# Start-up loads moved to ScalarE's queue and merged, transposes in merged PSUM banks, w2 in three loads: a dense layer with squared ReLU on one core

## Chip, cores, metric

One core of one Trainium2 chip. The metric is the device time of one execution in microseconds. Timed runs of one kernel differ by 0.5 us and more from each other, so comparisons use several runs taken on the same chip in the same rounds.

## The reference

```
h   = einsum("bsd,df->bsf", x, w1) + b1      # x: 1 x 2048 x 576, w1: 576 x 4608
r   = where(h > 0, h, 0)
out = einsum("bsf,fd->bsd", r * r, w2) + b2  # w2: 4608 x 576, everything bf16
```

## The kernel before

The rows of x are worked in four blocks of 512. For block 0, PE (TensorE) itself transposes x, because the first matmuls must start early; the other blocks come through DMA transposes. The contraction length 576 is 4 x 128 + 64. The first four 128-column groups of w1 ("w1n", loaded as four row blocks k = 0 to 3 of 128 KB) are used as full 128-row matmuls of half width (256 columns of x at a time, so that work can begin after two x tiles). The 64 left-over rows ("small rows", w1n8) close those groups. All other groups of w1 ("w1_h") are used in pairs of 64-row matmuls, the "64-row stage".

The parts that matter (cuts are marked):

```
WARM = [512] * 6 + [128]                    # warm-up matmuls on constants
...
load_x(nc.sync, 0)
load_x(nc.scalar, 1)
load_w1n(nc.sync, 0)
load_x(nc.scalar, 2)
load_w1n(nc.sync, 1)
load_x(nc.sync, 3)
for k in range(2, NK):                      # NK = 4
    load_w1n(nc.sync, k)
...
nc.gpsimd.dma_start(out=b1_rows[0:NFT, :], in_=...)   # bias 1
nc.gpsimd.dma_start(out=b2_col[:], in_=...)
...
def x_copies(h):                            # PSUM -> SBUF, half h of block 0
    hc = slice(h * HS, (h + 1) * HS)
    for k in range(NK):
        src = half_banks[h][k][:, 0, :]
        if k % 2 == 0: keep(nc.vector.tensor_copy(out=xT0[:, O + k, hc], in_=src))
        else:          keep(nc.scalar.copy(out=xT0[:, O + k, hc], in_=src))
    keep(nc.vector.tensor_copy(out=xT0[:, E3, hc], in_=half_banks[h][2][:, 1, :]))
...
# part(h, k): 4 half-width matmuls of x half h with w1 block k
for j in range(2):
    for k in range(NK): x_transpose(j, k)
for j in range(2): x_transpose(j, NK)
x_copies(0)
part(0, 0)
for k in range(NK + 1): x_transpose(2, k)
part(0, 1)
part(0, 2)
for k in range(NK + 1): x_transpose(3, k)
x_copies(1)
dup_windows(0)
part(0, 3)
part(1, 0)
make_b1T()                                  # transpose of bias 1
for k in range(1, NK): part(1, k)
...                                         # small rows, then the 64-row stage
for (j0, j1) in [(0, 1), (1, 2), (2, 4), ...]:
    load_w1(nc.sync, 0, j0, j1)
    load_w1(nc.sync, 1, j0, j1)
    if j0 == 0:
        load_w1n8(nc.sync, 0)               # the small rows
        load_w1n8(nc.sync, 1)
...
for c in (0, 2, 1, 3): load_w2(c)
```

Of the kernel before, what the change touches and what calls it, by code (L numbers as in the profile page):

```python
# [11 lines left out]
BF16 = mybir.dt.bfloat16  # L12
FP32 = mybir.dt.float32
# [4 lines left out]
def kernel(  # L18
# [9 lines left out]
    nc = tc.nc  # L28
    keep = tc.keep_in_program_order
    P = 128  # L30
# [3 lines left out]
    S, D = x2.shape  # L34
    F = w1.shape[1]
    NFT = F // P
    NC = D // H
    NK = NC // 2
    G = 4
    GW = G * P  # L40
# [4 lines left out]
    RT = SB // P  # L45
    DT = P
    DM = D - DT

    const = ctx.enter_context(tc.tile_pool(name="const", bufs=1))
# [6 lines left out]
    ps_h = ctx.enter_context(tc.tile_pool(name="ps_h", bufs=4, space=PSUM))  # L56
    ps_o = ctx.enter_context(tc.tile_pool(name="ps_o", bufs=4, space=PSUM))

    wps = ps_o.tile([P, 512], FP32, name="wps", tag="po")
    ones = nc.const_aps.tensor(1.0, [P, 512], BF16)  # L60
    WARM = [512] * 6 + [128]
    for i, n in enumerate(WARM):
        keep(nc.tensor.matmul(wps[:, 0:n], lhsT=ones[:, 0:P], rhs=ones[:, 0:n], start=True, stop=True))  # L63

    xs = const.tile([P, RT, D], BF16, name="x_sb")
    w1n = wpool.tile([P, NK, GW], BF16, name="w1n")
# [4 lines left out]
    def load_x(eng, rt):  # L71
        keep(eng.dma_start(out=xs[:, rt, :], in_=x2[rt * P:(rt + 1) * P, :]))

    def load_w1n(eng, k):
        keep(eng.dma_start(out=w1n[:, k, :], in_=w1[k * P:(k + 1) * P, 0:GW]))

    def load_w1n8(eng, h):
        src = w1[NK * P:D, 0:GW].rearrange("p (i h f) -> p i h f", h=2, f=P)
        keep(eng.dma_start(out=w1n8[h * H:(h + 1) * H, :, :], in_=src[:, :, h, :]))

    def load_w1(eng, h, j0, j1):
        keep(eng.dma_start(out=w1_h[h * H:(h + 1) * H, :, j0 * P:j1 * P],
                      in_=w1_v[:, :, GW + h * FH + j0 * P:GW + h * FH + j1 * P]))

    load_x(nc.sync, 0)
    load_x(nc.scalar, 1)
    load_w1n(nc.sync, 0)
    load_x(nc.scalar, 2)
    load_w1n(nc.sync, 1)
    load_x(nc.sync, 3)  # L90
    for k in range(2, NK):
        load_w1n(nc.sync, k)

    ident = const.tile([P, P], BF16, name="ident")
    make_identity(nc, ident[:])
    b1_rows = const.tile([P, P], BF16, name="b1_rows")
    nc.gpsimd.memset(b1_rows[:], 0.0)
    nc.gpsimd.dma_start(out=b1_rows[0:NFT, :], in_=b1.rearrange("(ft p) -> ft p", p=P))
    b2_col = const.tile([P, 1], BF16, name="b2_col")
    nc.gpsimd.dma_start(out=b2_col[:], in_=b2[DM:D].rearrange("(d o) -> d o", o=1))  # L100
    b2T = const.tile([P, 1], FP32, name="b2T")
    nc.gpsimd.tensor_copy(out=b2T[:], in_=b2_col[:])
    warm = const.tile([P, 1], FP32, name="warm")
    keep(nc.scalar.activation(out=warm[:], in_=nc.const_aps.tensor(0.0, [P, 1], FP32), func=ACT.Relu))

    E3, O, SPC, E = 0, 1, 5, 6
    LO_W = [O, O + 1, O + 2, O + 3, E, E + 1, E + 2, E3, SPC]
# [9 lines left out]
    def dup_windows(sb):  # L117
        xT = xT_blk[sb]
        keep(nc.vector.tensor_copy(out=xT[0:H, SPC:SPC + 4, :], in_=xT[H:P, E3:E3 + 4, :]))  # L119
        keep(nc.vector.tensor_copy(out=xT[H:P, SPC:SPC + 4, :], in_=xT[0:H, O:O + 4, :]))  # L120
# [7 lines left out]

    w2_sb = wpool.tile([P, NFT, D], BF16, name="w2_sb")
    w2_view = w2.rearrange("(ft p) d -> p ft d", p=P)  # L130
    W2CH = 9

    def load_w2(c):
        keep(nc.sync.dma_start(out=w2_sb[:, c * W2CH:(c + 1) * W2CH, :], in_=w2_view[:, c * W2CH:(c + 1) * W2CH, :]))
# [3 lines left out]
    alloc_xT(0)  # L138
    xT0 = xT_blk[0]
    HS = SB // 2  # L140
    tb_po = [ps_o.tile([P, 2, HS], BF16, name="tb", tag="po") for _ in range(2)]
    tb_ph = [ps_h.tile([P, 2, HS], BF16, name="tb", tag="ph") for _ in range(4)]
    half_banks = [tb_ph, None]

    def x_transpose(j, k):
        h, q = divmod(j, 2)
        qc = slice(q * P, (q + 1) * P)
        bank, slot, c0 = (half_banks[h][k], 0, k * P) if k < NK else (half_banks[h][2], 1, D - P)
        keep(nc.tensor.transpose(bank[:, slot, qc], xs[:, j, c0:c0 + P], ident[:]))  # L149

    def x_copies(h):
        hc = slice(h * HS, (h + 1) * HS)
        for k in range(NK):
            src = half_banks[h][k][:, 0, :]
            if k % 2 == 0:
                keep(nc.vector.tensor_copy(out=xT0[:, O + k, hc], in_=src))  # L156
            else:
                keep(nc.scalar.copy(out=xT0[:, O + k, hc], in_=src))
        keep(nc.vector.tensor_copy(out=xT0[:, E3, hc], in_=half_banks[h][2][:, 1, :]))


    b1T = const.tile([P, NFT], FP32, name="b1T")

    def make_b1T():
        b1T_ps = ps_o.tile([P, P], BF16, name="b1T_ps", tag="po")
        keep(nc.tensor.transpose(b1T_ps[:], b1_rows[:], ident[:]))  # L166
        keep(nc.vector.tensor_copy(out=b1T[:], in_=b1T_ps[:, 0:NFT]))

# [26 lines left out]
    def a_full(sb, order):  # L195
        xT = xT_blk[sb]
        banks = []
        for g in range(G):
            pool, tag = (ps_o, "po") if g < 2 else (ps_h, "ph")
            banks.append(pool.tile([P, SB], FP32, name="pn", tag=tag))  # L200

        def pair(i, start, stop):
            keep(nc.tensor.matmul(banks[2 * i][:], lhsT=w1n8[0:H, i, :], rhs=xT[0:H, SPC, :],  # L203
                             start=start, stop=stop, skip_group_check=order == "k_outer"))
            keep(nc.tensor.matmul(banks[2 * i + 1][:], lhsT=w1n8[H:P, i, :], rhs=xT[H:P, E3, :],  # L205
                             start=start, stop=stop, skip_group_check=order == "k_outer"))

        def full(g, k, start, stop):
            keep(nc.tensor.matmul(banks[g][:], lhsT=w1n[:, k, g * P:(g + 1) * P], rhs=xT[:, O + k, :],  # L209
                             start=start, stop=stop))  # L210

        if order == "rows_first":
            for i in (1, 0):
                pair(i, True, False)
            for g in (2, 3, 0, 1):
                for k in range(NK):
                    full(g, k, False, k == NK - 1)
                evac_h(sb, banks[g], g)
        else:
            if order == "k_outer":  # L220
                tb_new = [ps_h.tile([P, 2, HS], BF16, name="tb", tag="ph") for _ in range(2)]
                half_banks[1] = tb_new + tb_po

                def part(h, k):
                    hc = slice(h * HS, (h + 1) * HS)
                    for g in range(G):
                        keep(nc.tensor.matmul(banks[g][:, hc], lhsT=w1n[:, k, g * P:(g + 1) * P],  # L227
                                              rhs=xT[:, O + k, hc], start=(h == 0 and k == 0), stop=False,
                                              skip_group_check=True))

                for j in range(2):
                    for k in range(NK):
                        x_transpose(j, k)
                for j in range(2):
                    x_transpose(j, NK)
                x_copies(0)
                part(0, 0)
                for k in range(NK + 1):
                    x_transpose(2, k)
                part(0, 1)  # L240
                part(0, 2)
                for k in range(NK + 1):
                    x_transpose(3, k)
                x_copies(1)
                dup_windows(0)
                part(0, 3)
                part(1, 0)
                make_b1T()
                for k in range(1, NK):
                    part(1, k)  # L250
            else:
                for g in (2, 3, 0, 1):
                    for k in range(NK):
                        full(g, k, k == 0, False)
            for i in (1, 0):
                pair(i, False, True)
                evac_h(sb, banks[2 * i], 2 * i)
                evac_h(sb, banks[2 * i + 1], 2 * i + 1)
# [35 lines left out]
    for (j0, j1) in [(0, 1), (1, 2), (2, 4), (4, 6), (6, 8), (8, 10), (10, 12)]:  # L294
        load_w1(nc.sync, 0, j0, j1)
        load_w1(nc.sync, 1, j0, j1)
        if j0 == 0:
            load_w1n8(nc.sync, 0)
            load_w1n8(nc.sync, 1)
    load_xT(1)  # L300
    for (j0, j1) in [(12, 14), (14, 16)]:
        load_w1(nc.sync, 0, j0, j1)
        load_w1(nc.sync, 1, j0, j1)
    keep(nc.sync.dma_start(out=b2_bc[:], in_=b2.partition_broadcast(P)))
    for c in (0, 2, 1, 3):
        load_w2(c)
    load_xT(2)

    alloc_hT(0)
    a_full(0, "k_outer")  # L310
    a_rows(0, 12, 1)
    alloc_hT(1)
# [47 lines left out]
```

## Time and profile before

| | before |
|---|---|
| time, median of the first 3 runs | 290.84 us (290.69 to 291.06) |
| the profiled execution | 291.46 us, span 289.6 us |
| PE busy | 285.5 us, 99% |
| x tile 0 lands / first transpose | 3.72 / 3.77 us |
| w1 block 2 lands / first used (PE's weight load) | 6.47 / 6.69 us |
| w1 block 3 lands / first used (PE's weight load) | 7.05 / 7.46 us |
| first matmul of the 64-row stage on w1_h | 10.29 us |

Busy time of each engine, then the chain of work that ended last by engine, both from the page of before:

```profile
PE 285.5 (99%) x2027; PEld 139.9 (48%) x2032; DVE 78.6 (27%) x176; ACT 96.7 (33%) x154; POOL 2.3 (1%) x10
...
PE 98%; DMA 1%; issue 0%; DVE 0%
```

PE is the bound, so a gain must come from the start, where PE is not yet at work or works slowly. The chain of before in the first 11 us (cut at both ends; columns: start in us, length in us, what; it counts a matmul from the end of the one before, so its times lie up to 0.2 us after the starts that the text names):

```profile
0.73 2.99 DMA x_sb<-in_x_dram
3.73 0.04 issue
3.77 1.25 PE tb L149 x10
5.02 0.86 PE pn L227 x4
5.88 0.53 PE tb L149 x5
6.42 0.98 PE pn L227 x8
7.40 0.28 PE tb L149 x5
7.68 0.87 PE pn L227 x8
8.55 0.06 PE b1T_ps L166
8.61 1.31 PE pn L227 x12
9.92 0.32 PE pn L203
```

After tile 0 lands, this chain is PE alone. Five transposes take 0.53 us at 5.88 and 0.28 us at 7.40: PE runs at half speed until about 6.5 us. No line names a DMA of w1, and neither do PE's waits in the whole span:

```profile
PE wps L63 <- PEq L344: 0.8, 1, 0.8
PE pn L209 <- issue: 0.3, 2, 0.2
PE tb L149 <- DMA x_sb<-in_x_dram: 0.2, 1, 0.2
```

### The profile page before, as it was taken

The page shows a single profiled execution, that of the slowest core. Times are in us where ns is not written, and L with a number is a line of the kernel's source. Part 1 is how long each engine was busy: PE and PEld are TensorE (multiplying, and loading weights), DVE is VectorE, ACT ScalarE, POOL GpSimd, SP SyncE. Part 2 cuts the span into 40 slices and gives each one's busy share as a digit, 9 for nine tenths or more (in the row PEclk, how much of TensorE's full clock was granted, in tenths as well). Part 3 has the DMA queues.
Part 4 walks back from the last instruction along what each step waited for, and adds up shares of the span by engine and source line. Part 5 has one row for each costly group of instructions (what it writes and reads, how often), then busy time and mean ns, then how long its engine had stood idle before and what let it go on. Part 6 is the DMA issues. An engine that isn't in the chain of part 4 may idle for free.

```text
span 289.6 us, 4693 instructions
## 1 busy us (share of the span) xinstructions
PE 285.5 (99%) x2027; PEld 139.9 (48%) x2032; DVE 78.6 (27%) x176; ACT 96.7 (33%) x154; POOL 2.3 (1%) x10
## 2 busy tenths in 40 slices
PE   8999999999999999999999999999999999999996
PEld 5544444444444555555544444444444455555555
DVE  1644554444500200000015444444440001100001
ACT  2566666666500000000027666666670000000000
POOL 3000000000000000000000000000000000000000
PEclk9999999999999999999999999999999999999999
DMA  7999999400001200000000000000000110000000
GB/s 198 221 245 188 308 389 212 92 0 2 0 14 25 52 16 18 16 16 18 16 16 2 1 2 0 2 0 2 0 2 0 36 38 16 16 16 19 33 16 18
DMA packets 31605, 16.52 MB, mean 57 GB/s; under 512 B 15700, under 2 KB 31584, under 8 KB 31584
## 3 DMA queue, kind: packets, MB, share of 16 engines
q1 hardware_dynamic: 31232, 15.91, 22.3%
q10 hardware_dynamic: 288, 0.30, 0.4%
q8 instruction: 16, 0.26, 0.4%
q14 instruction: 5, 0.04, 0.0%
q0 software_dynamic: 64, 0.01, 0.0%
HBM read 11.36 MB, written 2.36 MB: 47 GB/s over the span
## 4 chain that ended last, share of the span: by engine, by line
PE 98%; DMA 1%; issue 0%; DVE 0%
PE ph L188 42%; PE po L289 38%; PE pt L270 11%; PE pn L209 4%; PE pn L227 1%; DMA x_sb<-in_x_dram 1%; PE tb L149 1%; PE ph L190 1%; PE pn L203 1%; DVE o_sb L291 0%; PE b1T_ps L166 0%; PE pn L205 0%
## 5 line engine op out<-in xcount | busy, mean ns | idle before, releaser
L190 PE MATMUL ph<-xTw,w_h 64*128 64x512 bf16 x576 | 124.6, 376 | 0.0
L188 PE MATMUL ph<-xTw,w_h 64*128 64x512 bf16 x576 | 124.6, 376 | 0.0
L289 PE MATMUL po<-w_sb,hT 128*128 128x448 bf16 (+2 forms) x612 | 109.4, 341 | 0.0
L176 ACT ACTIVATE r<-ph,b1T 128x512 bf16<-128x512 f32 x128 | 81.1, 685 | 41.6 <-PE ph L190 41.6
L188 PEld LDWEIGHTS <-w_h 64*128 64x128 bf16 x576 | 54.1, 94 | 68.3
L289 PEld LDWEIGHTS <-hT 128*128 128x128 bf16 x612 | 58.5, 98 | 51.0
L177 DVE TENSOR_TENSOR hT<-r 128x512 bf16<-128x512 bf16 x144 | 61.2, 426 | 75.9 <-ACT r L176 75.5
L190 PEld LDWEIGHTS <-w_h 64*128 64x128 bf16 x576 | 54.1, 94 | 0.0
L291 DVE TENSOR_TENSOR o_sb<-po,b_bc 128x448 bf16<-128x448 f32 (+2 forms) x17 | 10.2, 597 | 125.8 <-PE po L289 125.8
L270 PE MATMUL pt<-hT,w_sb 128*128 128x512 bf16 x142 | 31.3, 379 | 0.1
L176 ACT ACTIVATE r<-pn,b1T 128x512 bf16<-128x512 f32 x16 | 10.3, 688 | 61.0 <-PE pn L205 59.6
L270 PEld LDWEIGHTS <-w_sb 128*128 128x128 bf16 x144 | 14.1, 98 | 17.0
L273 ACT ACTIVATE oT<-pt,b2T 128x512 bf16<-128x512 f32 x4 | 2.8, 688 | 28.3 <-PE pt L270 28.3
L209 PE MATMUL pn<-xTw,w1n 128*128 128x512 bf16 x45 | 10.4, 379 | 0.4 <-issue 0.3
L209 PEld LDWEIGHTS <-w1n 128*128 128x128 bf16 x48 | 4.5, 98 | 6.0 <-issue 0.8
L227 PE MATMUL pn<-xTw,w1n 128*128 128x256 bf16 x32 | 4.6, 295 | 0.0
L63 PE MATMUL wps<-const-bfloat16-1.0 128*128 128x512 bf16 (+1 forms) x7 | 2.8, 582 | 0.8 <-PEq L344 0.8
L227 PEld LDWEIGHTS <-w1n 128*128 128x128 bf16 x32 | 3.3, 107 | 0.5
L156 DVE COPY xTw<-tb 128x256 bf16<-128x256 bf16 x4 | 1.1, 292 | 6.7 <-PE tb L149 6.7
L119 DVE COPY xTw<-xTw 64x2048 bf16<-64x2048 bf16 x4 | 2.8, 690 | 0.2
L120 DVE COPY xTw<-xTw 64x2048 bf16<-64x2048 bf16 x4 | 2.7, 687 | 0.1
L149 PE MATMUL tb<-ident,x_sb 128*128 128x128 bf16 x20 | 2.4, 288 | 0.2 <-DMA x_sb<-in_x_dram 0.2
(23 smaller groups left out, 15.2 us busy)
## 6 DMA issues: line engine op xcount, KB each, us to landing
w_sb<-in_w_dram SPq DMA_DIRECT2D x4, 1296.0 KB, 12.7
w_h<-in_w_dram SPq DMA_DIRECT2D x14, 288.0 KB, 6.2
out_dram<-o_sb SPq DMA_DIRECT2D x15, 112.0 KB, 1.7
w_h<-in_w_dram SPq DMA_DIRECT2D x4, 144.0 KB, 3.5
w1n<-in_w_dram SPq DMA_DIRECT2D x4, 128.0 KB, 3.9
out_dram<-ot SPq DMA_DIRECT2D x4, 128.0 KB, 2.0
x_sb<-in_x_dram ACTq DMA_DIRECT2D x2, 144.0 KB, 2.9
x_sb<-in_x_dram SPq DMA_DIRECT2D x2, 144.0 KB, 3.4
```

The source lines that it names most:

```text
L63: keep(nc.tensor.matmul(wps[:, 0:n], lhsT=ones[:, 0:P], rhs=ones[:, 0:n], start=True, stop=True))
L149: keep(nc.tensor.transpose(bank[:, slot, qc], xs[:, j, c0:c0 + P], ident[:]))
L176: keep(nc.scalar.activation(out=r[:], in_=bank[:], func=ACT.Relu, bias=b1T[:, ft:ft + 1], scale=1.0))
L177: keep(nc.vector.tensor_tensor(out=hTs[sb][:, ft, :], in0=r[:], in1=r[:], op=ALU.mult))
L188: keep(nc.tensor.matmul(bx[:], lhsT=w1_h[0:H, LO_C[i], jc], rhs=xT[0:H, LO_W[i], :], start=(i == 0), stop=(i == NC - 1)))
L190: keep(nc.tensor.matmul(by[:], lhsT=w1_h[H:P, UP_C[i], jc], rhs=xT[H:P, UP_W[i], :], start=(i == 0), stop=(i == NC - 1)))
L203: keep(nc.tensor.matmul(banks[2 * i][:], lhsT=w1n8[0:H, i, :], rhs=xT[0:H, SPC, :], start=start, stop=stop, skip_group_check=order == "k_o ...
L209: keep(nc.tensor.matmul(banks[g][:], lhsT=w1n[:, k, g * P:(g + 1) * P], rhs=xT[:, O + k, :], start=start, stop=stop))
L227: keep(nc.tensor.matmul(banks[g][:, hc], lhsT=w1n[:, k, g * P:(g + 1) * P], rhs=xT[:, O + k, hc], start=(h == 0 and k == 0), stop=False, s ...
L270: keep(nc.tensor.matmul(pt[:], lhsT=w2_sb[:, ft, DM:D], rhs=hT[:, ft, :], start=(i == 0), stop=(i == NFT - 1)))
L289: keep(nc.tensor.matmul(po[:, 0:d1 - d0], lhsT=hT[:, ft, jj * P:(jj + 1) * P], rhs=w2_sb[:, ft, d0:d1], start=(i == 0), stop=(i == NFT - 1)))
L291: keep(nc.vector.tensor_tensor(out=o_sb[:, d0:d1], in0=po[:, 0:d1 - d0], in1=b2_bc[:, d0:d1], op=ALU.add))
```

## The change

Its intent: take the issue of small loads off SyncE and GpSimd, feed PE with the third tile's transposes before the first matmuls so that it needn't wait for the first copies, and use fewer PSUM banks and fewer DMAs. The core of the diff (cut: pool names, the bookkeeping of banks):

```diff
-    WARM = [512] * 6 + [128]
+    WARM = [512] * 6 + [256]
...
     load_x(nc.sync, 0)
-    load_x(nc.scalar, 1)
-    load_w1n(nc.sync, 0)
-    load_x(nc.scalar, 2)
-    load_w1n(nc.sync, 1)
-    load_x(nc.sync, 3)
-    for k in range(2, NK):
-        load_w1n(nc.sync, k)
+    for rt in range(1, RT):
+        load_x(nc.scalar, rt)
+    for k0, k1 in [(0, 1), (1, 2), (2, NK)]:      # blocks 2 and 3 in one load
+        load_w1n(nc.sync, k0, k1)
...
-    nc.gpsimd.dma_start(out=b1_rows[0:NFT, :], ...)
-    nc.gpsimd.dma_start(out=b2_col[:], ...)
+    for h in range(2):                            # after the table load on ScalarE
+        load_w1n8(nc.scalar, h)
+    keep(nc.scalar.dma_start(out=b1_rows[0:NFT, :], ...))
...                                               # x_copies: half 0 all on VectorE,
...                                               # half 1: one merged copy on ScalarE
-                for j in range(2): ... x_transpose(j, k) ...
+                for j in range(2):
+                    x_transpose(j)
                 x_copies(0)
+                x_transpose(2)
                 part(0, 0)
-                x_transpose(2, k) ...
                 part(0, 1)
-                part(0, 2)
-                x_transpose(3, k) ...
+                x_transpose(3)
                 x_copies(1)
                 dup_windows(0)
+                part(0, 2)
                 part(0, 3)
...
-    W2CH = 9
+    W2CH = 12                                     # w2 in 3 loads, b2's column later, on SyncE
```

More of the change, by code (lines that the diff above doesn't have):

```diff
@@ L57 @@
     ps_o = ctx.enter_context(tc.tile_pool(name="ps_o", bufs=4, space=PSUM))
-    wps = ps_o.tile([P, 512], FP32, name="wps", tag="po")
+    wps = ps_h.tile([P, 512], FP32, name="wps", tag="ph")
     ones = nc.const_aps.tensor(1.0, [P, 512], BF16)
-    WARM = [512] * 6 + [128]
+    WARM = [512] * 6 + [256]
     for i, n in enumerate(WARM):
@@ L72, in load_x, with load_w1n @@
         keep(eng.dma_start(out=xs[:, rt, :], in_=x2[rt * P:(rt + 1) * P, :]))
-    def load_w1n(eng, k):
-        keep(eng.dma_start(out=w1n[:, k, :], in_=w1[k * P:(k + 1) * P, 0:GW]))
+    def load_w1n(eng, k0, k1):
+        src = w1[k0 * P:k1 * P, 0:GW].rearrange("(k p) f -> p k f", p=P)
+        keep(eng.dma_start(out=w1n[:, k0:k1, :], in_=src))
     def load_w1n8(eng, h):
@@ L83, in load_w1 @@
                       in_=w1_v[:, :, GW + h * FH + j0 * P:GW + h * FH + j1 * P]))
+    b1_rows = const.tile([P, P], BF16, name="b1_rows")
+    nc.vector.memset(b1_rows[:], 0.0)
     load_x(nc.sync, 0)
-    load_x(nc.scalar, 1)
-    load_w1n(nc.sync, 0)
-    load_x(nc.scalar, 2)
-    load_w1n(nc.sync, 1)
-    load_x(nc.sync, 3)
-    for k in range(2, NK):
-        load_w1n(nc.sync, k)
+    for rt in range(1, RT):
+        load_x(nc.scalar, rt)
+    for k0, k1 in [(0, 1), (1, 2), (2, NK)]:
+        load_w1n(nc.sync, k0, k1)
     ident = const.tile([P, P], BF16, name="ident")
     make_identity(nc, ident[:])
-    b1_rows = const.tile([P, P], BF16, name="b1_rows")
-    nc.gpsimd.memset(b1_rows[:], 0.0)
-    nc.gpsimd.dma_start(out=b1_rows[0:NFT, :], in_=b1.rearrange("(ft p) -> ft p", p=P))
-    b2_col = const.tile([P, 1], BF16, name="b2_col")
-    nc.gpsimd.dma_start(out=b2_col[:], in_=b2[DM:D].rearrange("(d o) -> d o", o=1))
-    b2T = const.tile([P, 1], FP32, name="b2T")
-    nc.gpsimd.tensor_copy(out=b2T[:], in_=b2_col[:])
     warm = const.tile([P, 1], FP32, name="warm")
     keep(nc.scalar.activation(out=warm[:], in_=nc.const_aps.tensor(0.0, [P, 1], FP32), func=ACT.Relu))
+    for h in range(2):
+        load_w1n8(nc.scalar, h)
+    keep(nc.scalar.dma_start(out=b1_rows[0:NFT, :], in_=b1.rearrange("(ft p) -> ft p", p=P)))
     E3, O, SPC, E = 0, 1, 5, 6
@@ L140, with x_transpose @@
     HS = SB // 2
-    tb_po = [ps_o.tile([P, 2, HS], BF16, name="tb", tag="po") for _ in range(2)]
-    tb_ph = [ps_h.tile([P, 2, HS], BF16, name="tb", tag="ph") for _ in range(4)]
-    half_banks = [tb_ph, None]
-    def x_transpose(j, k):
+    tb = [[ps_h.tile([P, 4, HS], BF16, name="tb", tag="ph") for _ in range(2)] for _ in range(2)]
+    PLACE = [(0, 0), (0, 1), (1, 0), (1, 1), (0, 2)]
+    T_ORDER = [0, 1, NK, 2, 3]
+    def x_transpose(j):
         h, q = divmod(j, 2)
-        qc = slice(q * P, (q + 1) * P)
-        bank, slot, c0 = (half_banks[h][k], 0, k * P) if k < NK else (half_banks[h][2], 1, D - P)
-        keep(nc.tensor.transpose(bank[:, slot, qc], xs[:, j, c0:c0 + P], ident[:]))
+        for k in T_ORDER:
+            bank, slot = PLACE[k]
+            c0 = k * P if k < NK else D - P
+            keep(nc.tensor.transpose(tb[h][bank][:, slot, q * P:(q + 1) * P], xs[:, j, c0:c0 + P], ident[:]))
     def x_copies(h):
         hc = slice(h * HS, (h + 1) * HS)
-        for k in range(NK):
-            src = half_banks[h][k][:, 0, :]
-            if k % 2 == 0:
-                keep(nc.vector.tensor_copy(out=xT0[:, O + k, hc], in_=src))
-            else:
-                keep(nc.scalar.copy(out=xT0[:, O + k, hc], in_=src))
-        keep(nc.vector.tensor_copy(out=xT0[:, E3, hc], in_=half_banks[h][2][:, 1, :]))
+        for k in (0, 1):
+            keep(nc.vector.tensor_copy(out=xT0[:, O + k, hc], in_=tb[h][0][:, k, :]))
+        if h == 0:
+            for k in (2, 3):
+                keep(nc.vector.tensor_copy(out=xT0[:, O + k, hc], in_=tb[h][1][:, k - 2, :]))
+        else:
+            keep(nc.scalar.copy(out=xT0[:, O + 2:O + 4, hc], in_=tb[h][1][:, 0:2, :]))
+        keep(nc.vector.tensor_copy(out=xT0[:, E3, hc], in_=tb[h][0][:, 2, :]))
     b1T = const.tile([P, NFT], FP32, name="b1T")
     def make_b1T():
-        b1T_ps = ps_o.tile([P, P], BF16, name="b1T_ps", tag="po")
+        b1T_ps = ps_h.tile([P, P], BF16, name="b1T_ps", tag="ph")
         keep(nc.tensor.transpose(b1T_ps[:], b1_rows[:], ident[:]))
@@ L198, in a_full @@
         for g in range(G):
-            pool, tag = (ps_o, "po") if g < 2 else (ps_h, "ph")
+            pool, tag = (ps_o, "po") if g < 2 or order == "k_outer" else (ps_h, "ph")
             banks.append(pool.tile([P, SB], FP32, name="pn", tag=tag))
@@ L220, in a_full @@
             if order == "k_outer":
-                tb_new = [ps_h.tile([P, 2, HS], BF16, name="tb", tag="ph") for _ in range(2)]
-                half_banks[1] = tb_new + tb_po
                 def part(h, k):
@@ L231, in a_full @@
                 for j in range(2):
-                    for k in range(NK):
-                        x_transpose(j, k)
-                for j in range(2):
-                    x_transpose(j, NK)
+                    x_transpose(j)
                 x_copies(0)
+                x_transpose(2)
                 part(0, 0)
-                for k in range(NK + 1):
-                    x_transpose(2, k)
                 part(0, 1)
-                part(0, 2)
-                for k in range(NK + 1):
-                    x_transpose(3, k)
+                x_transpose(3)
                 x_copies(1)
                 dup_windows(0)
+                part(0, 2)
                 part(0, 3)
@@ L296 @@
         load_w1(nc.sync, 1, j0, j1)
-        if j0 == 0:
-            load_w1n8(nc.sync, 0)
-            load_w1n8(nc.sync, 1)
     load_xT(1)
@@ L303 @@
         load_w1(nc.sync, 1, j0, j1)
+    b2_col = const.tile([P, 1], BF16, name="b2_col")
+    keep(nc.sync.dma_start(out=b2_col[:], in_=b2[DM:D].rearrange("(d o) -> d o", o=1)))
+    b2T = const.tile([P, 1], FP32, name="b2T")
+    nc.gpsimd.tensor_copy(out=b2T[:], in_=b2_col[:])
     keep(nc.sync.dma_start(out=b2_bc[:], in_=b2.partition_broadcast(P)))
-    for c in (0, 2, 1, 3):
+    for c in range(3):
         load_w2(c)
```

## The prediction

> What bounds it now. The page's busy shares have PE busy 285.5 of 289.6 us (99%); the chain of waits is 98% PE. From the first matmul of the 64-row stage (10.29 us) to the last (about 287 us), the view of PE's waits shows only two short gaps (0.3 us together), none for a DMA; w2 is first read at 76 us, its loads are issued by 35 us. So only the first 10.3 us can pay.
>
> The start, read in the chain and the timeline. x tile 0 is issued at 0.73 and lands at 3.72; the warm-up matmuls end at 3.61, so PE idles 0.17 us. Then PE is back to back: 20 transposes, 32 half-width matmuls and the bias transpose until 9.85, then 0.2 us at the change to 64-row matmuls. Until about 6.45 us it runs at half speed: 128-column transposes start 107 ns apart (later 55), half-width matmuls take 417 ns (later 272). The Trainium skill ("TensorE: Matmul & The Clock Gate", Part 1) says why: half clock until about one busy window of 3.4 us, with a free-running phase. The durations agree with the halving; one trace can't show that the phase varies.
>
> Check of the sum: 2.68 us at half clock do about 3200 columns; the remaining 7660 of 10,880 need about 3.3 us (an estimate from those spacings); 3.77+2.68+3.3 = 9.74, against 9.85 seen. So bank waits and copies cost at most 0.1 us today.
>
> What changes.
> - x tiles 1-3 on ScalarE's queue: tile 3 lands earlier, but its transposes (7.13 us) waited for nothing. Tile 0 still sets 3.7 us. The skill ("DMA: Bandwidth & Descriptors", Issuing engines are not separate DMA queues) says a second issuer saves only issue time, here 0.43 us an issue.
> - The third issue pushes the 1.28 us table load to 2.1-3.4; then two small w1 loads (0.62 us of issue each) and the bias at 4.9-5.4. The bias should land at 7.5-8 (2.2-3 us, as the other small loads), just ahead of its transpose at about 8.4: the thinnest margin. ScalarE's merged copy is due at about 7.2, after its issues.
> - SyncE sheds 1.3 us of small-w1 issue, so 64-row weights come earlier: PE never waited for them, gain 0.
> - Merged banks and tile 2's transposes ahead cover the 0.06 us wait for the first copy. First-half copies on VectorE (5 x 0.29) end at about 6.3, each ahead of its matmul. Window copies end at 9.4 instead of 9.7, still hidden.
> - Warm-up 128 columns longer: 0.11 us, inside the 0.17 us gap. Gain 0.
> - w2 in 3 loads, b2 later, GpSimd's queue empty: off the path.
>
> PE's columns are the same, so the 64-row stage should start at 10.1-10.3 instead of 10.29, the rest identical.
>
> Prediction: 290.6 us, 289.9 to 291.2. Faster by over 2%: 0.01; within 2%: 0.98; slower by over 2%: 0.01.
>
> What would show it. Right: first transpose at 3.7-3.8; fifteen transposes in one row; no PE gap over 0.1 us before 9.8 us; first 64-row matmul within 0.2 us of 10.29; later stages equal within 0.1 us. Bias step wrong: PE idle before the bias transpose, put down to its DMA. Copy step wrong: PE idle before the half-width matmuls, put down to DVE.
>
> What would make it wrong. If the half clock ends at another time, the total moves by half of that shift, up to about a microsecond either way, by chance or because the 0.17 us gap is closed. A late bias costs up to 1 us. Neither comes near 2% (5.8 us).

## More of the kernel before

The loads of the start (KB each, median us from issue to landing):

```profile
w1n<-in_w_dram SPq DMA_DIRECT2D x4, 128.0 KB, 3.9
...
x_sb<-in_x_dram ACTq DMA_DIRECT2D x2, 144.0 KB, 2.9
x_sb<-in_x_dram SPq DMA_DIRECT2D x2, 144.0 KB, 3.4
```

## The result

The changed kernel took 291.31 us (median of 4 runs, 290.91 to 291.77), before 290.95 us (4 runs, 290.69 to 291.31). Ratio 1.0012, 95% interval 0.9993 to 1.0031. (A ratio is the mean time of one kernel's fast runs over that of the other's in the same rounds, so it is not quite the ratio of the medians.) The class "within 2%" was right; the time lies 0.11 us above the predicted range and 0.7 us above the predicted value. Two more sets of runs gave 1.0007 (0.9995 to 1.0020) and 1.0021 (1.0007 to 1.0035): the changed kernel is not faster but about 0.2 to 0.55 us slower (+0.35, +0.22 and +0.55 us in the three sets; only the last is clear of noise by itself).

The page of after, same lines as for before:

```profile
PE 285.8 (99%) x2032; PEld 139.7 (48%) x2032; DVE 78.9 (27%) x179; ACT 96.0 (33%) x151; POOL 0.9 (0%) x7
...
PE 97%; DMA 2%; SPq 0%; DVE 0%; issue 0%
```

The chain of after in the first 11 us (cut at both ends):

```profile
1.67 0.42 SPq L76
2.09 0.04 issue
2.13 4.78 DMA w1n<-in_w_dram
6.91 0.05 issue
6.95 1.49 PE pn L221 x12
8.44 0.06 PE b1T_ps L163
8.49 1.31 PE pn L221 x12
9.80 0.32 PE pn L200
```

PE's waits in the trace of after, then the loads of w1 and x:

```profile
PE wps L63 <- PEq L334: 0.8, 1, 0.8
PE pn L221 <- DMA w1n<-in_w_dram: 0.2, 1, 0.2
```

```profile
x_sb<-in_x_dram ACTq DMA_DIRECT2D x3, 144.0 KB, 3.5
w1n<-in_w_dram SPq DMA_DIRECT2D x2, 128.0 KB, 3.4
w1n<-in_w_dram SPq DMA_DIRECT2D x1, 256.0 KB, 4.8
```

Three things are to be seen. The wait for x tile 0 is gone; the longer warm-up need not be the reason, since tile 0 landed 0.18 us earlier in this trace (3.55 us) and before_again below has no such wait with the short warm-up either. In its place a new wait has appeared, for the merged 256 KB load of blocks 2 and 3, which landed at 6.91 us; before, block 2 alone had landed at 6.47. And the chain no longer runs through PE before 6.95 us but through that load.

Yet this pair of traces says that after is 0.2 us *shorter* (spans 289.4 and 289.6), while the timed runs say it is longer. The traces differ in something that the diff doesn't name: the half speed ended at about 6.5 us in the trace of before and at 5.7 in that of after. From the first small-row matmul (9.85 us before, 9.73 after) to PE's end both traces take 277.03 us, so all that differs lies in the first 10 us. The same stretch takes 277.03 us in every trace but on_again (277.36) and three of the four held ones of section 5: when PE reaches the small rows decides the time.

### The profile page after: what moved, and what is told of

It reads as the page before. It is cut to its first block, busy times and chain, and to the rows that moved or that the text cites. A ratio compares the mean times of both kernels' runs of the same rounds, so it can differ in the third digit from the quotient of the medians.

```text
span 289.4 us, 4696 instructions
## 1 busy us (share of the span) xinstructions
PE 285.8 (99%) x2032; PEld 139.7 (48%) x2032; DVE 78.9 (27%) x179; ACT 96.0 (33%) x151; POOL 0.9 (0%) x7
## 4 chain that ended last, share of the span: by engine, by line
PE 97%; DMA 2%; SPq 0%; DVE 0%; issue 0%
PE ph L185 42%; PE po L278 38%; PE pt L259 11%; PE pn L206 4%; DMA w1n<-in_w_dram 2%; PE pn L221 1%; PE ph L187 1%; PE pn L200 1%; SPq L76 0%; SPq L72 0%; DVE o_sb L280 0%; PE b1T_ps L163 0%; PE pn L202 0%
## 5 line engine op out<-in xcount | busy, mean ns | idle before, releaser
L173 ACT ACTIVATE r<-pn,b1T 128x512 bf16<-128x512 f32 x16 | 10.3, 688 | 61.7 <-PE pn L202 60.3
L200 PE MATMUL pn<-xTw,w1n 64*128 64x512 bf16 x8 | 2.4, 379 | 0.0
L202 PE MATMUL pn<-xTw,w1n 64*128 64x512 bf16 x8 | 2.4, 379 | 0.0
```

The source lines that it names most:

```text
L173: keep(nc.scalar.activation(out=r[:], in_=bank[:], func=ACT.Relu, bias=b1T[:, ft:ft + 1], scale=1.0))
L200: keep(nc.tensor.matmul(banks[2 * i][:], lhsT=w1n8[0:H, i, :], rhs=xT[0:H, SPC, :], start=start, stop=stop, skip_group_check=order == "k_o ...
```

## The experiments

Three theories were set against each other. M: the merged load makes PE wait for block 2 until block 3 has landed too. L, and Q as a part of it: the new arrangement of loads as a whole brings w1's blocks later. C: the difference is only the moment of full clock, which differs between executions. "Difference" below is the mean time minus the mean of before in the same rounds.

| kernel (5 or 6 runs, held ones 4 or 5) | median us | difference us | ratio (95%) |
|---|---|---|---|
| after_again (the changed kernel) | 291.19 | +0.22 | 1.0007 (0.9995 to 1.0020) |
| after_third (the changed kernel) | 291.40 | +0.55 | 1.0021 (1.0007 to 1.0035) |
| after_split | 291.28 | +0.09 | 1.0003 (0.9990 to 1.0016) |
| after_reorder | 291.39 | +0.61 | 1.0021 (1.0008 to 1.0034) |
| before_merged | 291.89 | +0.87 | 1.0030 (1.0017 to 1.0042) |
| newloads_oldorder | 292.39 | +1.89 | 1.0068 (1.0046 to 1.0089) |
| oldloads_neworder | 290.64 | -0.37 | 0.9987 (0.9973 to 1.0001) |
| on_again (the same) | 290.71 | -0.08 | 0.9996 (0.9983 to 1.0008) |
| on_merged | 291.85 | +1.04 | 1.0034 (1.0021 to 1.0048) |
| on_x3act | 291.56 | +0.50 | 1.0016 (1.0003 to 1.0028) |
| on_small | 290.88 | +0.16 | 1.0004 (0.9992 to 1.0017) |
| on_mx | 291.77 | +0.74 | 1.0025 (1.0011 to 1.0039) |
| on_w2b2 | 290.90 | +0.05 | 1.0002 (0.9990 to 1.0014) |
| before_again (the kernel before) | 290.78 | +0.03 | 1.0003 (0.9991 to 1.0015) |

Each of these runs also left a trace of one execution. "Half speed ends" is where the spacing of the matmuls halves (half-width ones: 213 ns, then 109 ns). Landings are times from the span's start; "PE waits" is the longest wait of a matmul for w1. The traced execution is the first of the timed runs (for before, one more), so it can lie away from the median: 291.46 us for before, 290.97 for on_x3act, 291.35 for on_w2b2.

| trace | half speed ends | block 1 lands | block 2 usable | PE waits for w1 | 64-row stage starts |
|---|---|---|---|---|---|
| before | 6.5 | 5.86 | 6.47 | none | 10.29 |
| before_again | 6.1 | 4.81 | 6.04 | none | 10.04 |
| after | 5.7 | 5.38 | 6.91 | 0.2 | 10.18 |
| after_again | 6.5 | 4.92 | 6.36 | none | 10.16 |
| after_third | 5.6 | 5.79 | 7.08 | 0.4 | 10.35 |
| after_split | 6.6 | 5.77 | 6.22 | none | 10.18 |
| oldloads_neworder | 5.1 | 4.97 | 6.07 | none | 9.55 |
| on_again | 4.7 | 5.01 | 6.12 | none | 9.39 |
| on_merged | 4.9 | 5.24 | 7.44 | 1.1 | 10.71 |
| on_x3act | 4.0 | 5.88 | 6.53 | 0.6 (block 1) | 9.89 |
| on_small | 5.4 | 4.99 | 5.83 | none | 9.64 |
| on_mx | 3.7 | 6.53 | 7.55 | 1.3 (block 1) | 10.82 |
| on_w2b2 | 4.9 | 5.63 | 6.92 | 0.4 | 10.19 |
| before_merged | 3.9 | 5.47 | 7.36 | 1.3 | 10.91 |

One pattern in this table was not followed up. In the seven traces of the new order with old loads, or with one or two of the new ones (oldloads_neworder and on_again to on_w2b2), the half speed ended at 5.4 us or earlier; in the four of the changed kernel and its split form, and in after_reorder (6.6), at 5.6 us or later. The kernel before had 6.1 and 6.5, but before_merged 3.9. The text below takes this moment for chance. Whether a kernel's loads can move it was not tested, and where PE waits for no load, 1 us of it is worth about 0.5 us (an estimate from the halved spacing), as much as the differences in question.

### 1. The changed kernel again

No edit.

> The changed kernel once more, to see what its own runs differ by. Theory M (the merged load): the third and fourth w1 blocks now land together at about 6.9 us, PE waits 0.2 to 0.4 us for them before the half-width matmuls, and the 64-row stage cannot start before about 9.7 us however early the full clock comes; ratio to before 1.001 to 1.003. Rival C (the clock alone): the moment of the full clock moves between runs by up to a microsecond or more (6.51 us in the trace of before, 5.74 in that of after), and with it the start of the 64-row stage by half of that; ratio anything from 0.998 to 1.002. Both expect spans between 289.0 and 290.0.

Measured: +0.22 us; single runs 290.84 to 291.52. The trace shows no wait for w1, because the half speed lasted until 6.5 us and the merged load came at 6.36: PE simply reached it later. The stage still started at 10.16, as theory M's floor (9.7 for the first small-row matmul) and a late clock both allow. Taken alone this run tells nothing apart; what it shows is that landings and clock both move between executions of one kernel.

### 2. The merged load taken apart in the changed kernel

```diff
-    for k0, k1 in [(0, 1), (1, 2), (2, NK)]:
+    for k0, k1 in [(0, 1), (1, 2), (2, 3), (3, NK)]:
```

> The changed kernel with the third and fourth w1 blocks in two loads again. Theory M: the third block lands at about 6.4 and PE's wait for w1 falls from 0.35 us to under 0.1 us; the kernel is 0.2 to 0.3 us shorter than the changed one of the same rounds (ratio to before 0.999 to 1.000). Rival C: the wait is no part of the difference, the same time as the changed kernel within 0.1 us apart from chance. Rival Q (tile 3 of x on ScalarE's queue takes the DMA engines' turns from w1): the third block still lands at 6.8 or later, and the wait stays.

Measured: +0.09 us against +0.22 for the changed kernel of the same rounds. The 0.13 us between them is not clear of the noise, and the trace had a late clock (6.6 us), so it couldn't show the wait in question. Theory M's 0.2 to 0.3 us is not confirmed here. Three of its five runs were as slow as the changed kernel (291.28 to 291.51) and two were fast (290.68, 290.71).

### 3. The merged load alone in the kernel before

```diff
-    for k in range(2, NK):
-        load_w1n(nc.sync, k)
+    load_w1n(nc.sync, 2, NK)
```

> The kernel before with only the third and fourth w1 blocks merged in one load. Theory M: the merged block lands at about 7.0 us, PE waits for it 0.2 to 0.5 us, and the time goes up by 0.2 to 0.4 us over before (ratio 1.0007 to 1.0014). Rival C and rival Q: no wait, ratio 1.000.

Measured: +0.87 us, all five runs between 291.62 and 292.05. PE's wait for w1 in its trace:

```profile
PE pn L227 <- DMA w1n<-in_w_dram: 1.4, 2, 1.3
```

Theory M holds, and the cost is more than twice what was expected: the merged load landed at 7.36 us. That is later than block 3 alone in all eight traces with the blocks apart (6.24 to 7.32 us), so PE waits for more than block 3's own landing; why isn't shown. Rivals C and Q fall for this part.

### 4. Old loads, new order

The changed kernel with all its loads put back as they were before (x, w1 blocks, small rows, both biases, w2), so that only the banks, the order of transposes, the copies and the warm-up are new.

> The changed kernel's banks, transposes and copies with all loads as before. Theory M: no wait for w1's third block over 0.1 us, 0.2 to 0.3 us shorter than the changed kernel, ratio to before 0.999 to 1.000. If instead the new order costs something by itself (copies on VectorE late), PE waits for VectorE before half-width matmuls and the ratio is above 1.001.

Measured: -0.37 us; all five runs 290.47 to 290.78. So the new order is no loss by itself, and the loss must come with the loads, alone or together with the order.

### 5. The start held back, so that PE is at full clock when x lands

Four kernels (before, changed, changed with split load, old loads with new order) got dummy work on VectorE that writes x's tile before its loads may be issued, and 21 warm-up matmuls of full width. x tile 0 is then issued at 4.88 us:

```diff
-    WARM = [512] * 6 + [256]
+    WARM = [512] * 21
...
+    keep(nc.vector.memset(xs[:], 0.0))
+    for _ in range(2):
+        keep(nc.vector.tensor_tensor(out=xs[:], in0=xs[:], in1=xs[:], op=ALU.mult))
```

> The kernel before, all loads of the start held back about 5 us by dummy work on VectorE while 21 full warm-up matmuls run, so that TensorE has its full clock before x tile 0 lands: a tool, not a candidate. Theory C (the phase of the full clock makes the runs differ): its runs now agree within 0.15 us, where those of the kernel before spread over 0.5 us. With the full clock from the start, PE needs 4.6 us after tile 0 and the loads of w1 set the pace: a wait of 1 us or more in all for w1's blocks is expected in the trace. Time about 295 to 296 us.

> The changed kernel with the same hold. Theory L (the changed order of loads brings w1's blocks later, and that is what the change loses): 0.3 to 0.8 us slower than the held kernel before, with PE's wait longest at the merged block. Theory M gives 0.3 to 0.5 us from the merge alone. Rival C: no difference over 0.1 us between the two held kernels.

> The changed kernel with w1's third and fourth block apart, and the same hold. Theory M: as fast as the held kernel with the old loads and the new order. Theory L, with the small w1 rows, the bias and x tile 3 on ScalarE's queue taking the DMA engines' turns: no better than halfway between the held changed kernel and that one; 0.2 to 0.5 us slower than the held kernel with old loads and new order.

> Old loads, new banks and order of transposes, with the same hold. If the new order is worth anything by itself, it is 0.1 to 0.4 us faster than the held kernel before; it should be the fastest of the four.

Measured (medians): held before 296.65, held changed 295.49, held split 295.73, held old loads with new order 296.15. All four traces had full clock before x tile 0 landed (from 3.5 to 5.9 us on), and still the runs of one kernel spread over 0.8 us or more (split: 294.85 to 296.61). So rival C falls as the only cause of the spread: landings vary by themselves. Theory L's order of the four came out upside down, and the traces say why. With the full clock, the first small-row matmul of the changed kernel was the last of the four (13.95 us, against 13.05 for the split one, 13.11 for old loads with new order and 13.18 for before), 0.6 us of it idle in front of the merged load, as M says. But the three that started earlier had to wait for the loads of w1_h a few us later, 0.7 to 0.8 us each; from the first small-row matmul to PE's end they took 278.15 to 278.38 us, the held changed kernel 277.03. PE's waits for w1 up to 25 us in the held changed kernel, and in the held split kernel:

```profile
PE pn L224 <- DMA w1n<-in_w_dram: 0.6, 1, 0.6
```

```profile
PE ph L190 <- DMA w_h<-in_w_dram: 0.8, 1, 0.8
```

The early start was given back. This tool therefore answers when the stage can start, but not what that is worth: the 64-row weights set a second limit close behind the first. Unheld, on_again (the earliest start of all, 9.39 us) already touches it: its weight loads waited twice for w1_h, 0.4 us each at most, and the stretch after the first small-row matmul took 0.33 us more.

### 6. Each change of the loads alone, on old loads with new order

on_again is the base, run in the same rounds.

> Old loads with the new order once more, as the base of the next three. Theory L (the new order gains about 0.3 us, the new loads lose about 0.5): again 0.2 to 0.5 us under before, ratio about 0.9990. Rival C (the first time its five runs had an early clock by luck): ratio 0.9995 to 1.0005, and single runs up to 0.8 us above its fastest.

Measured: -0.08 us against before (-0.37 the first time). Both readings are under before, neither interval clears 1. By these means the new order is worth 0.1 to 0.4 us at old loads.

```diff
-    for k in range(2, NK):
-        load_w1n(nc.sync, k, k + 1)
+    load_w1n(nc.sync, 2, NK)
```

> Old loads and new order, with w1's third and fourth block merged alone. Theory M: 0.3 to 0.8 us slower than the base of this batch, and PE waits 0.3 us or more for the merged load if the clock is up before 5.5 us. Rival: under 0.1 us.

Measured: 1.11 us above the base (means), runs 291.75 to 292.04. Its chain:

```profile
2.62 4.82 DMA w1n<-in_w_dram
7.44 0.05 issue
7.49 1.48 PE pn L225 x12
8.97 0.06 PE b1T_ps L167
```

This is the changed kernel's chain, 0.5 us later: the merged load takes 4.8 us in both, but here x tile 3 is issued just before it on the same queue, so that it is issued at 2.62 instead of 2.13 us.

```diff
-    load_x(nc.sync, 3)
+    load_x(nc.scalar, 3)
```

> Old loads and new order, with x tile 3 on ScalarE's queue alone. Theory Q: tile 3's packets take turns with w1's second block, which lands at about 5.4 to 5.8 instead of 5.0; PE waits for it with an early clock; 0.1 to 0.3 us slower than the base. Rival: under 0.1 us, since the third block has as many bytes ahead of it as before.

Measured: 0.57 us above the base (means), in two groups (290.84 and 290.97; 291.56 to 291.63). The traced execution is one of the two faster ones (290.97), so the slow group has no trace. It waits for block 1, which landed at 5.88 us (base: 4.97 and 5.01):

```profile
PE pn L226 <- DMA w1n<-in_w_dram: 0.6, 1, 0.6
```

The mean is about twice what theory Q said. The Trainium skill ("DMA: Bandwidth & Descriptors", Queues, rings and completion order) says that each DMA engine takes turns between the queues for which it has work. The trace can be read that way: tile 3 is issued at 1.67 us, with block 1 (1.66), where the base issues it behind block 1, at 2.13. One trace doesn't show it, though: with tile 3 on SyncE's queue block 1 came as late in other executions (5.86 us in before, 5.63 in on_w2b2). Over the unheld traces it landed at 4.92 to 6.53 us, 5.70 in the mean, in the eight with tile 3 on ScalarE's queue, and at 4.81 to 5.86, 5.25 in the mean, in the eight with it on SyncE's. The direction fits theory Q; what made the slow group slow stays open.

```diff
+    for h in range(2):
+        load_w1n8(nc.scalar, h)
+    keep(nc.scalar.dma_start(out=b1_rows[0:NFT, :], in_=...))   # and not on SyncE, GpSimd
```

> Old loads and new order, with the small w1 rows and the bias on ScalarE's queue alone. If their small packets take turns with w1's third and fourth blocks, these land 0.1 to 0.4 us later and the time rises by as much; if not, the same as the base, and the 64-row weights land 0.5 us or more earlier than in the base, which should cost or gain nothing.

Measured: 0.24 us above the base in the mean, but four of its five runs lie at 290.76 to 290.99 and one at 291.48; blocks 2 and 3 landed no later (5.83 and 6.24). No cost is shown. The mechanism expected, later blocks, was not seen.

### 7. What stayed open: sums, w2 and b2, loads without the order, the wait itself

on_mx joins the two edits of the merge and of tile 3.

> Old loads and new order, with both the merge of w1's third and fourth block and x tile 3 on ScalarE's queue. If the merged load is issued and lands earlier because tile 3 no longer stands before it (about 6.4 to 6.9 us instead of 7.4), this is about 0.6 us slower than old loads with new order, not 1.7: about 291.3 us. If the two costs add, about 292.4 us.

Measured: +0.74 us, between the two expectations and nearer the first (291.66 in the mean); runs 291.0 to 292.19. In the trace even block 1 came at 6.53 us and PE waited 1.3 us for it. The costs don't add, but the reason given beforehand, an earlier merged load, isn't what this trace shows (7.55 us). Why the complete change, which has the small rows on ScalarE's queue as well, lands the merged load earlier (6.36 to 7.08 us in three traces) is not settled; with the same loads and the old order it came at 7.49 us, so chance has a large part in it.

```diff
-    nc.gpsimd.dma_start(out=b2_col[:], in_=...)     # now later, on SyncE
-    W2CH = 9
+    W2CH = 12
```

> Old loads and new order, with only b2's column later on SyncE's queue and w2 in three loads. Expected: nothing, 290.6 to 290.8 us, as old loads with new order. If the small b2 load on GpSimd's queue held up the first loads, up to 0.2 us faster.

Measured: +0.05 us: nothing clear of noise, and no gain. Its trace had an unmerged block 2 as late as 6.92 us; runs went from 290.65 to 291.35.

newloads_oldorder is the kernel before with all load changes (the load part of the diff above) and the old order.

> The kernel before with all the load changes and the old order of banks, transposes and copies. Theory L (loads lose, order gains): slower than the changed kernel, 291.4 to 291.9 us, with PE's wait for w1's blocks in the trace. If the new order is what loses, it is under 290.9 us.

Measured: +1.89 us, far over the expectation; four runs at 292.2 to 292.4, two at 293.8. Its trace shows a wait that nobody had named, beside the known one for the merged load (the two runs at 293.8 have no trace). ScalarE from 3.4 to 7 us, and PE's longest wait:

```profile
3.58 1.34 ACTq L80 DMA_DIRECT2D w1n<-in_w_dram  x2
5.02 0.74 ACTq L101 DMA_DIRECT2D b_rows<-in_b_dram  x1
5.80 0.65 ACT L155 COPY xTw<-tb 128x256 bf16<-128x256 bf16 x2 [2.15 <-DVE xTw L156]
```

```profile
PE pn L224 <- ACT xTw L155: 0.9, 1, 0.9
```

In the old order ScalarE makes two of the first half's copies. With the small loads in its program ahead of them, it is busy issuing until 5.76 us, and the copies that PE wants come 1.2 us later than before (5.80 instead of 4.63 us). (The bracket names VectorE as what ended the wait; but issuing isn't counted as busy, and the copy begins 0.04 us after the last issue ends.) The changed kernel gives all first-half copies to VectorE and has no such wait. In this trace, however, the copies did not set the time: the chain runs through the merged load, which landed at 7.49 us, after the wait for the copies was over.

```profile
2.13 5.36 DMA w1n<-in_w_dram
7.49 0.05 issue
7.53 0.61 PE pn L224 x4
```

In the mean the loads lose 1.9 us without the new order and 0.2 to 0.55 us with it; how much of that lies with the copies is not shown.

after_reorder leaves every load of the changed kernel alone and gives PE other work while the merged load is under way:

```diff
-                part(0, 2)
-                part(0, 3)
                 part(1, 0)
+                part(1, 1)
                 make_b1T()
-                for k in range(1, NK):
-                    part(1, k)
+                for k in range(2, NK):
+                    part(0, k)
+                    part(1, k)
```

> The changed kernel, all loads untouched, but the half-width matmuls of the second half's first two blocks and the bias transpose go ahead of those that need the merged load. If the wait for the merged block is the cost, PE's wait for it disappears and the time falls by 0.2 to 0.5 us under the changed kernel, to 290.7 to 291.0 us; a wait for VectorE's copies of up to 0.3 us may come in its place. If not the cost: 291.2 us or more.

Measured: +0.61 us, no better than the changed kernel, which by the expectation speaks against the wait as the cost. PE's wait for w1 is indeed gone, and one for VectorE's copies stands in its place, with the half speed lasting to 6.6 us in this trace:

```profile
PE pn L221 <- DVE xTw L151: 0.3, 1, 0.3
```

Since one wait was traded for another, this test does not decide what the wait for the merged load is worth in the changed kernel.

### 8. Both kernels once more

> The kernel before once more, for a second trace. If the full clock comes before about 5.5 us, PE waits up to 0.5 us for w1's second or third block and the 64-row stage starts at about 9.1 to 9.5 us; if it comes at 6 us or later, no wait and 9.6 to 9.9 us. Ratio 1.000.

> The changed kernel a third time. With a clock up before 5.7 us: PE waits 0.3 to 1 us for the merged block, and the 64-row stage starts about 2.8 us after that block lands; with a later clock: a wait under 0.4 us and a start at about 9.7 us. Ratio to before 1.0005 to 1.002.

Measured: before_again +0.03 us, half speed until 6.1 us, no wait, stage at 10.04 us. The expectation's upper branch said 9.6 to 9.9 us; the stage missed that by 0.14 us, and it fits only if the first small-row matmul (9.59) is meant. The early-clock branch was not seen, so whether before waits for w1 in other executions is still not shown. after_third: +0.55 us, with the interval clear of 1. Its chain:

```profile
2.13 4.95 DMA w1n<-in_w_dram
7.08 0.05 issue
7.13 1.49 PE pn L221 x12
8.61 0.06 PE b1T_ps L163
```

The stage starts at 10.35 us. In every trace of the new order in which PE waited for block 2 it starts 3.27 us after that block became usable: 6.91 and 10.18 (after), 7.08 and 10.35 (after_third), 7.44 and 10.71 (on_merged), 6.92 and 10.19 (on_w2b2). That constant is the work left: 24 half-width matmuls at 109 ns, the bias transpose and the small rows. In such executions the landing of that block sets the start of the stage, and the clock and the warm-up no longer matter. The order of the transposes matters through the constant alone: in the old order it is 3.55 us (7.36 and 10.91 in before_merged, 7.49 and 11.04 in newloads_oldorder), 0.28 us more, which is what the five transposes of tile 3 take there after block 2's matmuls.

## Why the prediction was right or wrong

Right:
- PE is the bound and only the first 10 us can pay. From the first small-row matmul to PE's end, before and after both take 277.03 us.
- Fifteen transposes stand in one row. The 0.17 us gap is gone too, but by luck as much as by the longer warm-up: tile 0 landed at 3.55 us in that trace, so the first transpose came at 3.60 us instead of 3.7 to 3.8.
- The bias was in time and w2, b2 and the empty GpSimd queue are off the path (on_w2b2: no difference clear of noise).
- "first 64-row matmul within 0.2 us of 10.29": 10.18, 10.16 and 10.35 us in three traces of the changed kernel. This forecast held, and yet it was not the gain it was taken for (see below).
- The clock moves between executions: half speed ended between 3.7 and 6.6 us in the unheld traces, and it can hide or show a wait.

Wrong:
- The step that failed is the sum "PE's columns are the same, so the 64-row stage should start at 10.1-10.3 instead of 10.29, the rest identical", as it was turned into 290.6 us. The start came as forecast (10.16 to 10.35 us) and the rest was identical, but 10.29 belonged to the profiled execution of 291.46 us, with its late clock, while 290.6 us is a gain of 0.25 us only against the median of 290.84. The span is the start of the stage plus 279.2 to 279.5 us in every unheld trace but on_again, and the 49 runs of before in the later rounds have a median span of 289.1 us. So the usual start of before is about 9.8 us (an estimate from these numbers), and a start at 10.1 to 10.3 us means 0.3 to 0.5 us lost, not 0.25 gained; measured was a loss of 0.2 to 0.55.
- What can hold the changed kernel at that start is missing from the list "What changes": it has no line for the merging of w1's blocks 2 and 3, although the diff has it. In both traces of the changed kernel in which the half speed ended before 6 us, PE waited for exactly this load; alone it costs 0.9 us (before_merged) and 1.1 us (on_merged against its base). The test "no PE gap over 0.1 us before 9.8 us" failed with it.
- "tile 3 lands earlier, but its transposes (7.13 us) waited for nothing" priced the move by what tile 3 gains and left out what others may lose. Alone it costs 0.57 us against its base in the mean (two runs 0.1 and 0.2 us, three over 0.8); a later block 1 fits that and is not shown to be the whole of it.
- "bank waits and copies cost at most 0.1 us today", so the new order was worth nothing more: by the means it is worth 0.1 to 0.4 us with the old loads (not clear of noise; 0.28 us by the traces when block 2 sets the pace), and over 1.3 us with the new ones (newloads_oldorder +1.89 us against +0.22 to +0.55 for the changed kernel in other rounds).
- Behind all of these stands one reading. That loads had slack ("waited for nothing" of tile 3, "PE never waited for them" of the 64-row weights) and that the stage starts at 10.29 us was taken from one execution in which the clock came late (6.5 us), so that PE was slow and the loads looked early. The slack was in that trace: block 2 landed 0.22 us (6.47 and 6.69 us) and block 3 0.41 us (7.05 and 7.46 us) ahead of first use (PE's weight load). If the clock comes 1 us earlier, PE gets there about 0.5 us sooner (an estimate from the half speed), more than the slack of either. A sign was on the page, too: the profiled execution took 291.46 us, the median run 290.84.

The sum as the runs have it: the loads lose (+1.9 us with the old order), the order gives most of it back, and +0.2 to +0.55 us is left, where the prediction had -0.25.

Not settled: how the 0.2 to 0.55 us of the complete change split between the merge, tile 3 and a later full clock, since neither splitting the load (0.13 us, not clear) nor giving PE other work (none) removed it; and why the costs of the single parts don't add.

The best version seen is old loads with new order: 290.64 and 290.71 us. It is 0.6 us under the changed kernel of the same rounds (290.63 against 291.22 in the mean) and under before by 0.1 to 0.4 us, which neither of its two intervals makes certain.

## What to carry to other kernels

Before calling a load slack, compare its landing with its first use, in an execution that is as fast as the median one, and take off what an earlier full clock would take. Merge two loads only if nothing waits for the first of them: here PE began on it only after the whole of it had landed (7.36 and 7.40 us in the chain of before_merged). A load moved to a second queue isn't free because its own consumer waits for nothing; ask which loads it now shares the DMA engines with, and what that engine's own program has to do behind the issue.

## What the Trainium skill lacked or had wrong

- "TensorE: Matmul & The Clock Gate", Part 1, gives the transition as varying by 500 ns from run to run; here half speed ended anywhere from 3.7 to 6.6 us over the unheld traces (14 in the table above). The same part's free-running window of about 3.4 us fits that width better. So does the clock record packed with the traces: its stretches of full clock are 283.31, 286.72 or 290.13 us long, which is steps of 3.41 us.
- The same page warns that the trace's clock events can be unreliable; it does not say that the start may lack them. In the trace of before the profile's granted clock reads 1.00 from 0.78 to 3.77 us, where full-width warm-up matmuls start 427 ns apart; later, matmuls of the same width start 216 ns apart (34 in 7.34 us). The spacing shows the half speed, the clock column did not: the record's first entry is full clock from 6.51 us, and the view counts the time without an entry as full.
- "DMA: Bandwidth & Descriptors", Rules for kernel authors, says to make transfers large and to coalesce small ones, and that section doesn't weigh a consumer that needs only the first part (another page advises splitting in general terms, without a number). Here one 256 KB load in place of two of 128 KB cost 0.9 to 1.1 us, since its first half was usable at 7.36 and 7.44 us, where block 2 alone had mostly come at 6.04 to 6.53.
- The same page, Issuing engines are not separate DMA queues, says that a second issuer saves only issue time, and that the DMAs interleave. It lacks a number for what this can cost another load: with x tile 3 on the second queue, w1's block 1 landed at 5.70 us in the mean of eight traces, against 5.25 in eight with it on the first; the two groups overlap.
- No page puts a number on what DMA issues on ScalarE cost its own copies (sequencer cycles for a single issue are given, their effect on the engine's other work is not): two small loads and a bias of 9 KB occupied it from 3.58 to 5.76 us, and PE waited 0.9 us for a copy behind them (a wait that a later load hid in that trace).
